# A gated attention and dense decode step on one Trainium2 core: the second weight load waits for a GpSimd fill

## The chip, the cores and the metric

The kernel runs on one core of one Trainium2 chip. The metric is the time of one execution on the device in microseconds (us), as the median of several runs. The profile is one further execution of the same program, taken by the hardware profiler.

## The reference, cut to what matters

All arrays are float32. A token of 512 features for each of two batch rows goes through a sliding block of attention over cached keys and values, and through a dense layer with Mish; a sigmoid gate mixes the two.

```python
W = min(4096, max(256, Sk // 4))              # Sk = 32768, so 4096 cached positions
q = (x @ wq) split into 32 heads of 128       # x: 2 x 512, wq: 512 x 4096
k, v = the last W positions of the caches, 8 kv heads, each for 4 query heads
p = softmax(q . k * 128 ** -0.5)
a = (p . v, heads joined) @ wo                # wo: 4096 x 512
h = x @ w1 + b1                               # w1: 512 x 1792
b = (h * tanh(softplus(h))) @ w2              # w2: 1792 x 512
g = sigmoid(sum(x * gate_w))
return g * a + (1 - g) * b
```

Nearly all bytes are the cached keys and values (8 kv heads of 8 MiB each) and the weights wq, wo, w1 and w2. Each is read once.

## The kernel before, in words

The work is one stream of loads from HBM into SBUF with the computation hung on it. Three buffers of 128 partitions x 16384 floats (8 MiB, the pool `stream`) take turns. The first holds all of `wq`, the next eight fills hold one kv head each (keys in the first half, values in the second), and the last two hold w1 with parts of w2 and wo (`w12`), and the rest of wo.

Nearly all loads are issued by SyncE, in the order in which `load` (L69 to L75) and the later lines call them, and each goes over the same hardware queue to the 16 DMA engines of the core. At the start SyncE issues:

- `wqh`, the first 2048 columns of `wq` (1 MiB; 8 KiB for each partition), at L73;
- `wqt`, the other 14336 columns (7 MiB; 56 KiB for each partition), at L73;
- `small`, 16 KiB with the token, the gate's weights and a bias, at L79, into the tile `sm`;
- the first two kv heads, at L73, into the two buffers that are still free.

The third kv head must wait until TensorE has used `wq` up, and each later load until the buffer that it takes has been read.

GpSimd starts with constants. In the order in which the program runs them: the identity matrix (masks.py), `ones` (L97), zeros for the padded token `x32` (L100; the profile calls the tile x), the first steps of a folding matrix (L87, L89), zeros for the padded queries `qz` (L103), more folding, zeros for `padded` (L106), and two small products of the folding matrix (L92, L111). Then it copies the token out of `sm` into `x32` (L101), for which it must wait for the load `small`, and multiplies token and gate weights (L118).

TensorE takes `x32` and `wq` to the queries (`queries`, L137), in two halves. VectorE puts them into the zeroed `qz` (L149). For each kv head follow the scores (L157), a maximum (L160), the exponentials (L162), a transposition (L169, L170) and the product with the values (L181). Behind the eighth head come the first layer of the dense part (`hidden`, L252), the output projections (L342) and, with the last load of w2, the final sums (L352). VectorE copies them to `res` (L385), and SyncE stores `res` (L386).

A scheduler places the instructions of each engine. Where `pin` (`tc.keep_in_program_order`) stands around an instruction, it keeps its place in the program's order.

Of the kernel before, what the change touches and what calls it, by code (L numbers as in the profile page):

```python
# [55 lines left out]
def decode_kernel(ctx: ExitStack, tc: tile.TileContext, res, stored, small, wqh, wqt, kv_in, w12, wo, w2, *rest):  # L56
    *parts, before, behind, out = rest
    nc = tc.nc
# [8 lines left out]
    loads = []  # L67

    def load(name, *parts):  # L69
        t = stream.tile([P, 2 * CHUNK], F32, tag="s", name=name)  # L70
        x = 0
        for cols, src in parts:
            loads.append(nc.sync.dma_start(t[:, x : x + cols], src))  # L73
            x += cols
        return t  # L75

    wq_t = load("wq", (HEAD, wqh), (2 * CHUNK - HEAD, wqt))
    sm = const.tile([P, SMALL], F32, name="sm")
    loads.append(nc.sync.dma_start(sm, small))  # L79
    xT = sm[:, : (DC + SLOTS) * B].rearrange("p (c b) -> p c b", b=B)  # L80
    gw = sm[:, (DC + SLOTS) * B : (DC + SLOTS) * B + DC]
    b1 = sm[:, (DC + SLOTS) * B + DC :]
# [17 lines left out]
    nc.gpsimd.memset(x32, 0.0)  # L100
    nc.gpsimd.tensor_copy(x32[:, :, ::RS], xT)  # L101
    qz = const.tile([P, HKV, BN * (Q + REP)], F32, name="qz")
    nc.gpsimd.memset(qz, 0.0)  # L103
    sizes = (HQ * Q, CUTS[1] * Q, (FC - CUTS[1]) * WIDE, WIDE)
    padded = const.tile([P, sum(sizes)], F32, name="padded")
    nc.gpsimd.memset(padded, 0.0)  # L106
# [182 lines left out]
    for kv in range(HKV):  # L289
        t = load(f"kv{kv}", (2 * CHUNK, kv_in[kv]))  # L290
        p = scores(kv, t[:, :CHUNK])
        ms = tops() if kv == HKV - 1 else None
        pT = turned(kv, p)
        values(kv, pT, t[:, CHUNK:], 0, 1)
        if kv == HKV - 1:
            kf, kl = factors(ms)
        values(kv, pT, t[:, CHUNK:], 1, 2)
        if kv == HKV - 1:
            r = shares(kl)
        values(kv, pT, t[:, CHUNK:], 2, NT)  # L300
    w12_t = load("w12", (AHEAD + CUTS[1] * D, w12))

    def flat(src, cuts, size):
# [4 lines left out]
    x = (WO[-1] - WO[0]) * REP * D  # L308
# [16 lines left out]
    x = 0  # L325
# [3 lines left out]
    x = AHEAD + CUTS[1] * D  # L329
# [31 lines left out]
    first = WO[0] * REP  # L361
# [19 lines left out]
    for ld in loads[-8:]:  # L381
        tc.add_manual_dep(landed.ins, ld.ins.name,
                          mybir.DependencyInfo(mybir.DependencyClass.Sync, mybir.DependencyReason.DATA),
                          reason="SyncE sees the last loads land ahead of the store")
# [5 lines left out]
                      reason="the store reads the copy")  # L390
# [72 lines left out]
```

## Time and profile before

| what | value |
|---|---|
| median of 3 runs | 218.84 us (218.77 to 218.93) |
| the profiled execution's own time | 219.24 us |
| its span, from the first instruction to the last | 217.4 us |
| bytes read from HBM | 91.24 MB |
| busy share of the span: TensorE, VectorE, ScalarE, GpSimd | 53%, 10%, 7%, 5% |
| mean granted TensorE clock | 0.867 |

The 219.24 us are the profiled execution timed as the runs are; the span lies inside it and leaves 1.84 us outside. Times in the views count from the span's start. The timeline shows a start, a duration, the engine, its source line and what is written from what; behind it, in brackets, the idle time of the engine and what ended it. SPq and POOLq are the queues of SyncE and GpSimd, on which DMA issues stand with the time that the engine needs to issue them, not with that of the transfer. The rows of windows give for a stretch of time its length, then the busy time of each engine with its count, the granted clock of TensorE, the busy share of the 16 DMA engines and the GB/s that they moved. A transfer is counted in the stretch in which it starts, with all its bytes, so short stretches go far above or below the mean once the pieces are large. The pieces of `wqh` are 8 KiB, and those of `wqt` 56 KiB.

### The profile page before, as it was taken

The page shows a single profiled execution, that of the slowest core. Times are in us where ns is not written, and L with a number is a line of the kernel's source. Part 1 is how long each engine was busy: PE and PEld are TensorE (multiplying, and loading weights), DVE is VectorE, ACT ScalarE, POOL GpSimd, SP SyncE. Part 2 cuts the span into 40 slices and gives each one's busy share as a digit, 9 for nine tenths or more (in the row PEclk, how much of TensorE's full clock was granted, in tenths as well). Part 3 has the DMA queues.
Part 4 walks back from the last instruction along what each step waited for, and adds up shares of the span by engine and source line. Part 5 has one row for each costly group of instructions (what it writes and reads, how often), then busy time and mean ns, then how long its engine had stood idle before and what let it go on. Part 6 is the DMA issues. An engine that isn't in the chain of part 4 may idle for free.

```text
span 217.4 us, 1857 instructions
## 1 busy us (share of the span) xinstructions
PE 115.5 (53%) x826; PEld 34.6 (16%) x826; DVE 21.5 (10%) x32; ACT 15.5 (7%) x34; POOL 11.4 (5%) x34
## 2 busy tenths in 40 slices
PE   0000798477046708543670754296165509669995
PEld 0000322112011102110210111012011101213333
DVE  0000000010001140100114010000501000260100
ACT  2000001111001100200110020002002000301001
POOL 8000000000000000000000000000000410100200
PEclk9999999979758995995898599769859976999799
DMA  8797988898899889998999899989998999989894
GB/s 362 338 507 338 582 386 386 386 570 386 386 398 567 386 377 410 543 398 386 410 497 434 386 422 458 470 386 422 437 482 386 434 449 421 427 377 475 381 409 162
DMA packets 2752, 91.38 MB, mean 420 GB/s; under 512 B 566, under 2 KB 646, under 8 KB 954
## 3 DMA queue, kind: packets, MB, share of 16 engines
q1 hardware_dynamic: 2602, 91.24, 97.4%
q8 instruction: 6, 0.10, 0.2%
q0 software_dynamic: 144, 0.05, 0.1%
HBM read 91.24 MB, written 0.04 MB: 420 GB/s over the span
## 4 chain that ended last, share of the span: by engine, by line
DMA 79%; PE 14%; ACT 2%; SPq 2%; DVE 1%; issue 1%; POOL 1%; ACTq 0%
DMA kv<-in_kv 61%; DMA w<-in_w 17%; PE sc L157 7%; PE o L181 5%; ACT p L162 1%; PE fin L352 1%; SPq L314 1%; DVE mx L160 1%; PE pp L169 1%; ACT pT L170 1%; POOL wo L310 1%; SPq L73 0%; SPq L327 0%; SPq L79 0%; DVE res L385 0%
## 5 line engine op out<-in xcount | busy, mean ns | idle before, releaser
L157 PE MATMUL sc<-kv,qz 128*32 128x512 f32 x256 | 44.6, 860 | 53.6 <-DMA kv<-in_kv 53.6
L181 PE MATMUL o<-kv,pT 128*32 128x512 f32 x256 | 29.5, 596 | 5.8 <-ACT pT L170 5.8
L137 PE MATMUL qp<-wq,x 128*32 128x512 f32 x64 | 12.1, 802 | 23.2 <-POOL x L101 23.2
L157 PEld LDWEIGHTS sc<-kv,qz 128*32 128x32 f32 x256 | 9.9, 151 | 87.6 <-DMA kv<-in_kv 60.2
L160 DVE TENSOR_REDUCE mx<-sc 128x1 f32<-128x512 f32 x8 | 5.5, 691 | 112.4 <-PE sc L157 112.4
L162 ACT ACTIVATE p<-sc,mx 128x512 f32<-128x512 f32 x8 | 5.5, 687 | 131.3 <-DVE mx L160 131.3
L169 PE MATMUL pp<-ident,p 128*128 128x128 f32 x32 | 5.2, 287 | 12.1 <-ACT p L162 12.1
L181 PEld LDWEIGHTS o<-kv,pT 128*32 128x32 f32 x256 | 7.3, 109 | 20.9 <-issue 13.2
L310 POOL MEMSET wo<- 128x1536 f32 x1 | 1.4, 1378 | 143.5 <-PE o L181 143.5
L191 DVE TENSOR_REDUCE od<-om 128x256 f32<-128x1024 f32 x4 | 7.6, 1911 | 0.1
L137 PEld LDWEIGHTS qp<-wq,x 128*32 128x32 f32 x64 | 2.5, 137 | 29.1 <-POOL x L101 23.2
L342 PE MATMUL acc<-wo,padded 128*32 128x512 f32 x56 | 7.1, 607 | 0.0
L188 DVE TENSOR_TENSOR om<-o,pick 128x1024 f32<-128x1024 f32 x4 | 4.9, 1224 | 19.3 <-PE o L181 19.3
L169 PEld LDWEIGHTS pp<-ident,p 128*128 128x128 f32 x32 | 3.4, 141 | 18.6 <-ACT p L162 18.6
L170 ACT COPY pT<-pp 128x512 f32<-128x512 f32 x8 | 4.7, 585 | 6.2 <-PE pp L169 6.2
L342 PE MATMUL acc<-w,padded 128*32 128x512 f32 x22 | 4.5, 884 | 0.4 <-DVE padded L235 0.4
L252 PE MATMUL hp<-w,x 128*32 128x512 f32 (+1 forms) x30 | 3.6, 540 | 1.8 <-DMA w<-in_w 1.8
L342 PEld LDWEIGHTS acc<-wo,padded 128*32 128x32 f32 x56 | 2.3, 117 | 4.6 <-issue 3.4
L252 PE MATMUL hp<-wo,x 128*32 128x512 f32 x6 | 2.7, 592 | 0.0
L126 DVE RECIPROCAL g<-g 128x2 f32<-128x2 f32 x1 | 0.2, 165 | 22.5 <-POOL g L125 22.5
L352 PE MATMUL fin<-w,padded 128*32 128x128 f32 x56 | 2.1, 277 | 0.3 <-DMA w<-in_w 0.3
L143 PE MATMUL qt<-ident,qs 128*128 128x128 f32 x8 | 1.3, 287 | 1.4 <-ACT qs L140 1.4
(71 smaller groups left out, 35.6 us busy)
## 6 DMA issues: line engine op xcount, KB each, us to landing
wq<-in_wqt SPq DMA_DIRECT2D x1, 7168.0 KB, 21.5
w<-in_w SPq DMA_DIRECT2D x1, 6144.0 KB, 40.6
wo<-in_wo SPq DMA_DIRECT2D x1, 5120.0 KB, 30.8
wo<-in_wo SPq DMA_DIRECT2D x1, 2048.0 KB, 35.2
wq<-in_wqh SPq DMA_DIRECT2D x1, 1024.0 KB, 5.0
w<-in_w SPq DMA_DIRECT2D x1, 1024.0 KB, 37.2
w<-in_w SPq DMA_DIRECT2D x1, 512.0 KB, 35.4
w<-in_w SPq DMA_DIRECT2D x1, 256.0 KB, 21.2
```

Of the source, the lines that this page charges most:

```text
L137: nc.tensor.matmul(qp[Q * k : Q * k + Q, :], x32[:, c, :], w[:, c, k, :], start=(c == 0), stop=(c == DC - 1))
L157: nc.tensor.matmul(sc[Q * j : Q * j + Q, :], qz[:, kv, m * Q : m * Q + Q], t[:, (m * NJ + j) * 512 : (m * NJ + j + 1) * 512], start=(m == ...
L160: nc.vector.tensor_reduce(mx[:, kv : kv + 1], sc, axis=AX.X, op=ALU.max, negate=True)
L162: nc.scalar.activation(p, sc, AF.Exp, bias=mx[:, kv : kv + 1], accum_out=ls[:, kv : kv + 1])
L169: pin(nc.tensor.transpose(pp[:, c, :], p[:, c * P : (c + 1) * P], ident))
L170: nc.scalar.copy(pT, pp)
L181: pin(nc.tensor.matmul(o[Q * j : Q * j + Q], pT[:, c, Q * j : Q * j + Q], t[:, (c * NJ + j) * 512 : (c * NJ + j + 1) * 512], start=(c == 0 ...
L188: nc.vector.tensor_tensor(ov, pair[0].rearrange("p k (m d) -> p k m d", m=BN), pick[:, None, :, None].to_broadcast([P, 2, BN, DH]), op=ALU ...
L191: nc.vector.tensor_reduce(od[:, kv - 1 : kv + 1], ov.rearrange("p k m d -> p k d m"), axis=AX.X, op=ALU.add)
L252: nc.tensor.matmul(hp[Q * j : Q * j + Q, :n], x32[:, c, :], w[:, :n], start=(c == 0), stop=(c == (DC + SLOTS if j in away else DC) - 1))
L342: return nc.tensor.matmul(acc[Q * j : Q * j + Q, :], lhsT, rhs, start=(n_col[j] == 1), stop=(n_col[j] == n))
L352: nc.tensor.matmul(fin[Q * j : Q * j + Q, :], lhsT[:, y : y + Q], rhs[:, j * P : (j + 1) * P], start=(done[0] == 0), stop=(done[0] == n_fi ...
```

## The change

SyncE issues `wqt`, the second load of `wq`, only when GpSimd has written the zeros of `qz`. The dependency is written for `loads[1:3]`, which are `wqt` and `small`; both also keep their places in the program's order, as all loads made by `load` now do.

```diff
         for cols, src in parts:
-            loads.append(nc.sync.dma_start(t[:, x : x + cols], src))
+            loads.append(tc.keep_in_program_order(nc.sync.dma_start(t[:, x : x + cols], src)))
             x += cols
...
     sm = const.tile([P, SMALL], F32, name="sm")
-    loads.append(nc.sync.dma_start(sm, small))
+    loads.append(tc.keep_in_program_order(nc.sync.dma_start(sm, small)))
...
     qz = const.tile([P, HKV, BN * (Q + REP)], F32, name="qz")
-    nc.gpsimd.memset(qz, 0.0)
+    blank = nc.gpsimd.memset(qz, 0.0)
+    for ld in loads[1:3]:
+        tc.add_manual_dep(ld.ins, blank.ins.name,
+                          mybir.DependencyInfo(mybir.DependencyClass.Sync, mybir.DependencyReason.DATA),
+                          reason="the first load has the queues for itself at first")
```

No instruction changes its place on any engine. On SyncE the one difference is a wait, at the start of the program, where `wq` and the first kv heads are loaded; lines marked - are the kernel before, lines marked + the changed one.

```order
 L73 DMA wq<-in_wqh 128x2048
-L73 DMA wq<-in_wqt 128x14336
+L73 DMA wq<-in_wqt 128x14336 [waits Pool_49]
 L79 DMA sm<-in_small 128x32
 L73 DMA kv_169<-in_kv 128x16384
```

Pool_49 is the semaphore that GpSimd counts up. Only `wqt` carries the wait; `small` and the first two kv heads stand behind it on SyncE and so come later too. On GpSimd the order in the changed kernel is that of before (behind the diff the line numbers are 4 higher):

```order
L100 MEMSET x_93 128x224
L87 TENSOR_TENSOR fold<-ident 128x32 [waits Pool_49]
L103 MEMSET qz 128x1152
L89 TENSOR_TENSOR fold<-fold,ident 128x32 [waits Pool_49]
L110 MEMSET padded 128x1744
L89 TENSOR_TENSOR fold<-fold,ident 128x32 [waits Pool_49]
L92 TENSOR_TENSOR key<-fold 128x8 [waits Pool_49]
L115 COPY padded<-fold 128x2
L101 COPY x_93<-sm 128x14 [waits DMAHW2_49]
```

The zeros of `qz` stand ahead of the copy that waits for `small`, so the two waits, SyncE's for GpSimd and GpSimd's for the load, don't close a circle.

## The prediction

> **What bounds the kernel now.** I began with the page's chain of the work that ended last, its shares by engine, and then the same chain in order of time (start, duration, what).
>
> ```profile
> DMA 79%; PE 14%; ACT 2%; SPq 2%; DVE 1%; issue 1%; POOL 1%; ACTq 0%
> ```
>
> ```profile
> 2.10 39.91 DMA kv<-in_kv
> ...
> 175.89 37.22 DMA w<-in_w
> 213.10 0.14 issue
> 213.24 2.25 PE fin L352 x64
> 215.49 0.03 issue
> 215.51 0.29 DVE res L385
> ```
>
> The chain is loads for four fifths of its length. It steps onto TensorE only where a buffer must be read before the next load is issued. Whether the loads really leave no gap there is read from the windows, over the whole middle of the span:
>
> ```profile
> 5.50:20.00 14.50, 0.00 (x0) 0.00 (x0) 0.00 (x0) 0.00 (x0) 0.00 (x0) 1.00 0.98 423
> 20.00:60.00 40.00, 24.71 (x148) 7.76 (x148) 1.43 (x6) 2.73 (x6) 0.77 (x4) 0.92 0.99 427
> 60.00:100.00 40.00, 20.33 (x136) 5.26 (x136) 4.49 (x4) 2.73 (x6) 0.00 (x0) 0.80 1.02 443
> 100.00:140.00 40.00, 19.24 (x136) 5.10 (x136) 4.49 (x4) 2.73 (x6) 0.00 (x0) 0.84 0.98 423
> 140.00:170.00 30.00, 18.58 (x128) 5.09 (x132) 4.49 (x4) 2.73 (x6) 0.00 (x0) 0.80 1.03 446
> 170.00:212.00 42.00, 29.54 (x214) 9.78 (x210) 6.17 (x12) 2.67 (x8) 6.11 (x15) 0.88 0.96 412
> ```
>
> The DMA share (last but one) stays between 0.96 and 1.03, and TensorE is busy for at most 0.70 of a row (29.54 of 42.00). So the kernel is one unbroken stream of loads, from about 2 us to 213.10, and then a tail: 217.4 - 213.1 = 4.3 us, in which the change touches nothing. The time moves by as much as the stream begins earlier or later, or by a hole in it, and by nothing else. All that matters is whether the change does one of these two in the first 6 us.
>
> **The wait's length.** Here are SyncE's issues at the start, and GpSimd's fill, from the timeline.
>
> ```profile
> 0.72 0.39 SPq L73 DMA_DIRECT2D wq<-in_wqh  x1
> 1.17 0.41 SPq L73 DMA_DIRECT2D wq<-in_wqt  x1
> ...
> 1.79 1.05 POOL L103 MEMSET qz<- 128x1152 f32 x1
> ```
>
> ```profile
> 1.62 0.43 SPq L79 DMA_DIRECT2D sm<-in_small  x1
> 2.10 0.77 SPq L73 DMA_DIRECT2D kv<-in_kv  x1
> ...
> 2.91 0.46 SPq L73 DMA_DIRECT2D kv<-in_kv  x1
> ```
>
> The fill ends at 1.79 + 1.05 = 2.84. What a wait of SyncE for a GpSimd fill costs beyond that is in the chain near the end, where a load waits for the fill at L310:
>
> ```profile
> 171.35 1.39 POOL wo L310
> 172.74 0.02 issue
> 172.75 0.89 SPq L314
> ```
>
> That is 0.02 us. So the issue of `wqt` moves from 1.17 to 2.86, by 1.69 us. Behind it on SyncE stand `small`, and the first two kv heads. With their own issue times kept (0.41, 0.43, 0.77, 0.46 and the gaps of 0.04 to 0.05 between them), `small` is issued at 3.3, the heads at 3.8 and 4.6. GpSimd doesn't wait for SyncE ahead of its copy of the token, so its fill isn't late.
>
> **What is queued behind the wait.** GpSimd waits for `small`, and TensorE for GpSimd's copy.
>
> ```profile
> 22.89 0.20 POOL L101 COPY x<-sm 128x14 f32<-128x14 f32 x1 [17.74 <-DMA sm<-in_small]
> ```
>
> `small` lands just ahead of 22.89 because 7 MiB of `wqt` stand ahead of it on the same queue, not because of its issue at 1.62. Issued at 3.3 it is still far ahead of its turn, and the first head, which follows it, too. The third head must wait until TensorE, which starts behind that copy, has used `wq` up, and so doesn't see the start. All this costs nothing as long as the queue holds `wqt` in time; what hides the 1.69 us is therefore `wqh` alone, the one load that is on the engines then.
>
> **Does `wqh` cover the wait?** Two things are needed: when the engines run out of `wqh`, and when they get `wqt`. The first is seen in short windows, since a piece of 56 KiB counted at its start lifts a slice far above the rate of the 8 KiB pieces.
>
> ```profile
> 4.70:4.80 0.10, 0.00 (x0) 0.00 (x0) 0.02 (x1) 0.00 (x0) 0.04 (x1) 1.00 1.35 573
> 4.80:4.90 0.10, 0.00 (x0) 0.00 (x0) 0.10 (x1) 0.00 (x0) 0.08 (x1) 1.00 1.71 737
> ...
> 5.30:5.40 0.10, 0.00 (x0) 0.00 (x0) 0.00 (x0) 0.00 (x0) 0.00 (x0) 1.00 2.66 1147
> 5.40:5.50 0.10, 0.00 (x0) 0.00 (x0) 0.00 (x0) 0.00 (x0) 0.00 (x0) 1.00 0.00 0
> ```
>
> The first engine goes over from `wqh` to `wqt` at 4.80 or just behind it, the last by 5.40; the middle is 5.10. The second is read from the two loads of the trace that find idle engines: `wqh` itself, and the store at the end.
>
> ```profile
> 1.60:1.70 0.10, 0.00 (x0) 0.00 (x0) 0.00 (x0) 0.10 (x1) 0.10 (x2) 1.00 0.00 0
> 1.70:1.80 0.10, 0.00 (x0) 0.00 (x0) 0.00 (x0) 0.10 (x1) 0.10 (x2) 1.00 0.42 164
> ```
>
> ```profile
> 215.83 0.35 SPq L386 DMA_DIRECT2D out<-res  x1
> ```
>
> ```profile
> 216.50:216.60 0.10, 0.00 (x0) 0.00 (x0) 0.00 (x0) 0.00 (x0) 0.00 (x0) 1.00 0.00 0
> 216.60:216.70 0.10, 0.00 (x0) 0.00 (x0) 0.00 (x0) 0.00 (x0) 0.00 (x0) 1.00 0.09 26
> 216.90:217.00 0.10, 0.00 (x0) 0.00 (x0) 0.00 (x0) 0.00 (x0) 0.00 (x0) 1.00 0.15 36
> ```
>
> From issue to first piece it is 1.70 - 0.72 = 0.98 to 1.08 us for `wqh`, and 216.60 - 215.83 = 0.77 to 0.87 us for the store. For `wqt`, issued at 2.86, that gives first pieces at 3.63 to 3.94, at least 0.86 us ahead of 4.80. But not all engines start at once, as the rate at the start shows:
>
> ```profile
> 1.50:2.00 0.50, 0.00 (x0) 0.00 (x0) 0.00 (x0) 0.50 (x1) 0.50 (x3) 1.00 0.19 66
> 2.00:2.50 0.50, 0.00 (x0) 0.00 (x0) 0.00 (x0) 0.00 (x1) 0.50 (x1) 1.00 0.31 82
> 2.50:3.00 0.50, 0.00 (x0) 0.00 (x0) 0.00 (x0) 0.00 (x0) 0.50 (x3) 1.00 0.76 295
> 3.00:3.50 0.50, 0.00 (x0) 0.00 (x0) 0.00 (x0) 0.00 (x0) 0.50 (x2) 1.00 0.97 410
> ```
>
> The full 410 GB/s are there only from 3.00, so the last engine may have got its first piece as late as 2.9, 2.2 us behind the issue. If `wqt` ramps up in the same way, its last engine gets work at 2.86 + 2.2 = 5.06. That is ahead of the middle, 5.10, and of 5.40, at which the last engine of `wqh` is through; the first engine of `wqh` would stand idle for 5.06 - 4.80 = 0.26 us only if it were the last one of `wqt`. I put the hole at 0, with 0.26 us as its upper bound. Without this cover the price would be the whole 1.69 us.
>
> **What the change can give.** In the kernel before the issues of `wqt`, `small` and the first head (1.17 to 2.87) fall into the slow ramp of `wqh`. By 3.00, (66 + 82 + 295) x 0.5 = 221 KB were moved, which take 0.54 us at 410 GB/s; since the first piece, 1.30 us had gone by. So 0.76 us of the stream are lost in the ramp. The changed kernel leaves `wqh` alone until 2.86. If the ramp comes from the issues behind it, up to 0.76 us come back; if it is the queue's own start, nothing does. The store, with nothing issued behind it, put all its pieces out from 216.60 to 217.00, which speaks for the first; but it runs at the end, on a queue long in use, and its pieces are small. Even in the better case `wqt` ramps up in its turn, now with `small` and the heads behind it: its last engine gets work at 5.06 in place of 5.40, a gain of 0.34, and its first engine can change over at 4.80 - 0.76 = 4.04, the full gain. The upper bound is the mean of the two, 0.55 us. I take 0.2 us, a little over half the way from 0 to the 0.34 us of the last engine: the last engine sets the end if all 16 carry the same bytes, as I assume, and the trace does not tell the two reasons apart.
>
> **The sum.** The profiled execution took 219.24 us. Less 0.2 for the ramp, plus 0 for the hole, it would be 219.04. It stands 0.40 us above the median of the runs (218.84), so the median of the changed kernel would be 218.64, say 218.65. That is 0.09% faster. About 0.2% (0.44 us) is what a measurement of this kernel can tell from no change, so I count my forecast as no change.
>
> **The rivals.**
>
> *The change does nothing.* Each engine has the pieces of `wqh` ahead of those of `wqt` on its list in any case, and the slice ahead of 4.80 (573 GB/s in 0.1 us, 7 pieces of 8 KiB) shows no piece of 56 KiB. Then `wqt` could not hold `wqh` up, the wait is hidden, and the time is 218.84. Against it stands only the slow ramp that coincides with the issues. The Trainium skill states a rule of this kind in "DMA: Bandwidth & Descriptors", under "Two DMAs through the same engine are not ordered": within one queue of one DMA engine, descriptors start in order. The trace agrees with it, by the slices around 4.80.
>
> *The ramp goes, and the gain is large.* With the full 0.55 us the time is 219.24 - 0.55 - 0.40 = 218.29; from a gain of 0.44 us on it counts as faster. For it speaks the issue time of the first head, 0.77 us where `wqt` and `small` took 0.41 and 0.43: something was held up in just this stretch. Against it speaks that the first pieces of `wqh`, in company, start 0.98 us behind their issue, little later than the 0.77 us of the store, and that `wqt` must ramp up as well. The landing of `wqh` gives a cross-check.
>
> ```profile
> wq<-in_wqh SPq DMA_DIRECT2D x1, 1024.0 KB, 5.0
> ```
>
> The Trainium skill, in "DMA: Bandwidth & Descriptors" under "Anatomy of one DMA", fits a load issued by GpSimd by itself as about 2.0 us and its bytes at 436 GB/s; as an estimate for this one that is 2.0 + 2.4 = 4.4 us, and the sum by it would be a gain of 0.6 us, where no run here shows `wqh` alone.
>
> *A hole between the two loads (slower).* Its place is the seam at 4.80 to 5.40. `wqt` is now prepared while the engines are busy, with `small` and two heads right behind it, and no row of this trace shows how long that takes with nothing else queued. If the ramp took twice as long as that of `wqh` (0.98 to the first piece, then 2 x 1.2 to the last engine), the last engine would have work at 2.86 + 3.38 = 6.24, a hole of 6.24 - 5.40 = 0.84 us, and the time would be 218.84 + 0.84 = 219.68. It decides against the change when the last engine's delay passes 5.40 + 0.44 - 2.86 = 2.98 us, against the 2.2 us seen. For it speaks only that the state isn't shown; against it the two idle-engine loads, both with a first piece within 1.08 us.
>
> **How the numbers follow.** My forecast, the wait hidden with a gain of under 0.44 us, has 0.45; that nothing happens, 0.23; the large gain, 0.20; the hole, 0.12. The first two both lie within 0.2%: 0.68. Faster by more, 0.20; slower by more, 0.12. The range begins at 218.25, just under the full gain, and ends at 219.10, which is 218.84 and the bound of the hole, 0.26; the slower rival and a little of the faster one stay out, under 2 in 10.
>
> **What would show it.** In the profile after, the issue of `wqt` should stand at about 2.86 with a wait for GpSimd at L103, the GB/s at 1.50 to 3.00 should be higher than before if the ramp came from the issues behind, the seam should lie at 4.6 to 5.4 with no slice of low rate ahead of it, the copy at L101 should start between 22.3 and 22.9, and all later landings should be moved by that amount. I am wrong if a stretch of 0.5 us between 3.0 and 5.5 falls clearly under 410 GB/s (the hole), if the copy at L101 comes over 0.4 us earlier (the large gain), or if it keeps its place and the end moves all the same, which would mean that the stream is disturbed later.

## The result, and the profile after

The changed kernel takes 219.34 us (median of 14 runs, 218.88 to 221.08) against 218.83 us for the kernel before (14 runs, 218.71 to 219.27). The ratio is 1.0026, with a 95% interval from 1.0013 to 1.0038: slower by 0.51 us. The runs also lie further apart than before, so what was added is not the same in each execution.

The profiled execution of the changed kernel took 219.28 us. It is near its median, while that of the kernel before (219.24) lies 0.4 us above its own. The two spans are both 217.4 us, so the two profiles don't show the 0.51 us as a difference in length; they show what differs at the start. SyncE's issues and the fill, from the timeline of the changed kernel:

```profile
0.73 0.39 SPq L73 DMA_DIRECT2D wq<-in_wqh  x1
1.80 1.05 POOL L103 MEMSET qz<- 128x1152 f32 x1
2.87 0.33 SPq L73 DMA_DIRECT2D wq<-in_wqt  x1
3.25 0.43 SPq L79 DMA_DIRECT2D sm<-in_small  x1
```

`wqt` is issued at 2.87 instead of 1.17, right behind the fill. The rates while `wqh` is read (windows; the last two columns are the share of the DMA engines and GB/s):

```profile
1.50:2.00 0.50, 0.00 (x0) 0.00 (x0) 0.00 (x0) 0.50 (x1) 0.50 (x3) 1.00 1.44 246
2.00:2.50 0.50, 0.00 (x0) 0.00 (x0) 0.00 (x0) 0.00 (x1) 0.50 (x1) 1.00 0.68 98
2.50:3.00 0.50, 0.00 (x0) 0.00 (x0) 0.00 (x0) 0.00 (x0) 0.50 (x2) 1.00 0.51 213
3.00:3.50 0.50, 0.00 (x0) 0.00 (x0) 0.00 (x0) 0.00 (x0) 0.50 (x2) 1.00 0.97 410
```

More pieces start ahead of 2.00 (246 GB/s against 66), but the share of 1.44 tells that they are long: 1.44 x 0.5 us x 16 engines are 11.5 us for 15 pieces of 8 KiB (246 GB/s over 0.5 us), 0.77 us each, where 410 GB/s on 16 engines make it 0.32. They began sooner and took longer. The full rate is there at 3.00, as before.

The next view shows what differs where the engines go over from `wqh` to `wqt`. The second pieces of `wqt`, 56 KiB each, begin when the first ones are done. One such piece in 0.5 us is 115 GB/s, so GB/s over 115 counts the pieces, and I take each for one engine, since the trace doesn't name the engine of a piece. Before:

```profile
6.50:7.00 0.50, 0.00 (x0) 0.00 (x0) 0.00 (x0) 0.00 (x0) 0.00 (x0) 1.00 0.26 115
7.00:7.50 0.50, 0.00 (x0) 0.00 (x0) 0.00 (x0) 0.00 (x0) 0.00 (x0) 1.00 3.97 1720
7.50:8.00 0.50, 0.00 (x0) 0.00 (x0) 0.00 (x0) 0.00 (x0) 0.00 (x0) 1.00 0.00 0
```

The changed kernel:

```profile
6.50:7.00 0.50, 0.00 (x0) 0.00 (x0) 0.00 (x0) 0.00 (x0) 0.00 (x0) 1.00 1.06 459
7.00:7.50 0.50, 0.00 (x0) 0.00 (x0) 0.00 (x0) 0.00 (x0) 0.00 (x0) 1.00 1.87 803
7.50:8.00 0.50, 0.00 (x0) 0.00 (x0) 0.00 (x0) 0.00 (x0) 0.00 (x0) 1.00 1.32 573
```

Before, 1 + 15 engines are done with their first piece by 7.50. In the changed kernel 4 engines are ahead of the rest, and 5 come behind 7.50. The trace's records of single transfers say why: around this place 16 pieces are under way but for 0.02 us, so no engine stands empty between the loads to speak of; the first pieces of `wqt` begin at 4.81 to 5.17 (before 4.85 to 5.33), but 7 of the 16 take 2.34 to 2.61 us, where the median piece has 2.12 and the longest first piece of before 2.26. They are drawn out. The last piece of `wqt` ends at 22.59 instead of 22.25, and `small` lands behind it.

```profile
wq<-in_wqt SPq DMA_DIRECT2D x1, 7168.0 KB, 20.0
wq<-in_wqh SPq DMA_DIRECT2D x1, 1024.0 KB, 4.8
sm<-in_small SPq DMA_DIRECT2D x1, 16.0 KB, 19.8
```

```profile
23.14 0.21 POOL L101 COPY x<-sm 128x14 f32<-128x14 f32 x1 [17.97 <-DMA sm<-in_small]
```

`wqh` lands 4.8 us behind its issue, 0.2 sooner than before. `wqt` has 1.70 us less for its bytes and needs only 1.5 us less (20.0 against 21.5). GpSimd's copy, which waits for `small`, starts at 23.14 instead of 22.89. Behind that the program runs as before; its last wait in the chain is still the same load, issued and landed within 0.1 us of where it stood, and the tail has the length it had:

```profile
175.88 37.28 DMA w<-in_w
213.17 0.14 issue
213.30 2.23 PE fin L356 x64
215.56 0.29 DVE res L389
```

### The profile page after: what moved, and what is told of

The parts are those of the page before. It is cut to its first block, busy times and chain, and to the rows that moved or that the text cites. A ratio compares the mean times of both kernels' runs of the same rounds, so it can differ in the third digit from the quotient of the medians.

```text
span 217.4 us, 1857 instructions
## 1 busy us (share of the span) xinstructions
PE 113.8 (52%) x826; PEld 33.6 (15%) x826; DVE 21.6 (10%) x32; ACT 15.5 (7%) x34; POOL 11.4 (5%) x34
## 4 chain that ended last, share of the span: by engine, by line
DMA 78%; PE 14%; ACT 2%; POOL 2%; SPq 2%; DVE 1%; issue 1%; ACTq 0%; POOLq 0%
DMA kv<-in_kv 61%; DMA w<-in_w 17%; PE sc L161 7%; PE o L185 5%; ACT p L166 1%; PE fin L356 1%; DVE mx L164 1%; SPq L318 1%; PE pp L173 1%; ACT pT L174 1%; POOL wo L314 1%; POOL qz L103 0%; SPq L331 0%; SPq L79 0%; DVE res L389 0%
## 5 line engine op out<-in xcount | busy, mean ns | idle before, releaser
L346 PE MATMUL acc<-wo,padded 128*32 128x512 f32 x56 | 6.4, 596 | 1.4 <-DMA wo<-in_wo 1.4
L346 PE MATMUL acc<-w,padded 128*32 128x512 f32 x22 | 2.8, 601 | 0.4 <-DVE padded L239 0.4
L346 PEld LDWEIGHTS acc<-wo,padded 128*32 128x32 f32 x56 | 1.6, 109 | 6.2 <-DMA wo<-in_wo 3.2
```

What stands on the lines that cost most here:

```text
L346: return nc.tensor.matmul(acc[Q * j : Q * j + Q, :], lhsT, rhs, start=(n_col[j] == 1), stop=(n_col[j] == n))
```

## The experiments

Theory A is that the wait costs at the seam, where the engines go over from `wqh` to `wqt`: `wqt` is issued too short a time ahead of it. Theory B puts the cost on the company, `small` and the two heads, which are now issued ahead of the seam too. C looks for it behind 23 us; D says that a wait there costs as such; G and H came up on the way. The kernel before was run again beside each of the five groups of experiments: its medians were 218.85 (x1 to x4), 218.89 (x5 to x8), 218.91 (x9 to x12), 218.90 (x13 to x16) and 218.86 us (x17, x18).

In what follows the *lead* of a kernel is the time from the issue of `wqt` to the start of its first piece on the first engine, in its profile. The *drawn-out* pieces are those of the 16 first ones that take over 0.15 us longer than the median piece, from the trace's records of single transfers.

**x1: the changed kernel again.** No edit.

> The changed kernel once more, for a second profile of it. Theory A (the seam): wqt, prepared late on busy engines, reaches the last engines late; some of its first 56 KiB pieces take 2.3 us and more where the kernel before has 2.12, the copy at L101 comes 0.2 to 0.6 us later than 22.89, and the median is again 219.1 to 219.6. Theory C (elsewhere): the copy at L101 stands within 0.1 us of 22.89 in this profile, and the time goes behind 23 us.

219.56 us (7 runs, 219.03 to 219.98), ratio 1.0031 (1.0019 to 1.0043). Two drawn-out pieces, the longest of 2.73 us; the copy at L101 starts at 23.43. As A has it; C, with the copy in its old place, falls.

**x2 and x3: the company alone, and `wqt` alone.** In x2 only `small` waits, with the heads behind it; in x3 `wqt` waits as in the change, and `small` for the next fill.

```diff
 x2
-    for ld in loads[1:3]:
+    for ld in loads[2:3]:
 x3
-    for ld in loads[1:3]:
+    for ld in loads[1:2]:
...
-    nc.gpsimd.memset(padded, 0.0)
+    blank2 = nc.gpsimd.memset(padded, 0.0)
+    for ld in loads[2:3]:
+        tc.add_manual_dep(ld.ins, blank2.ins.name, ...
```

> wqt is issued at 1.17 as in the kernel before, and only small, with the two heads behind it, waits for the zeros of qz. Theory A (the lateness of wqt itself at the seam costs): as before or a little under, 218.6 to 218.9, first pieces of wqt at 2.12 us. Theory B (the company costs: small and the heads, issued behind wqt while the engines are busy with wqh, hold up its pieces): still slower, 219.1 to 219.5, with the long first pieces of wqt.

> wqt waits for the zeros of qz as in the changed kernel, and small with the heads behind it waits for the next fill, padded, to about 4.55. Theory A: as slow as the changed kernel, 219.1 to 219.6, with long first pieces of wqt. Theory B: wqt is alone from 2.87 to 4.55 and is ready in time, so 218.6 to 218.9 and pieces of 2.12 us.

x2: 219.08 us, ratio 1.0012 (1.0003 to 1.0021), no drawn-out piece, copy at 22.74, and the profiled execution took 218.91. x3: 219.56 us, ratio 1.0031 (1.0019 to 1.0043), 5 drawn-out pieces. Taking the company away from `wqt` didn't help, and holding the company alone cost a third of what x1 lost (0.23 of 0.71 us). B falls as the cause. The 0.2 us of x2 fit neither theory well.

**x4: the wait made longer.** `wqt`, `small` and the heads wait for the fill of `padded`; the loop of the change stands behind it.

```diff
-    blank = nc.gpsimd.memset(qz, 0.0)
+    nc.gpsimd.memset(qz, 0.0)
...
-    nc.gpsimd.memset(padded, 0.0)
+    blank = nc.gpsimd.memset(padded, 0.0)
```

> wqt, small and the heads wait for the fill of padded, so wqt is issued at about 4.57, 1.70 us later than in the changed kernel. Theory A: the cover is gone, first pieces at 5.5 to 6.8 us instead of 4.8 to 5.2, and each further 0.1 us of wait costs 0.1 us: 220.6 to 221.1. Theory B: the same hole of the issue time alone, from 5.2 to about 5.6, and the held pieces, 219.7 to 220.3. Theory C: no more than the changed kernel, 219.3.

220.34 us, ratio 1.0067 (1.0055 to 1.0079): 1.5 us over before, under A's 220.6 and over B's 220.3 by little. Here there is a true hole (timeline, windows):

```profile
4.57 0.34 SPq L73 DMA_DIRECT2D wq<-in_wqt  x1
```

```profile
5.00:5.50 0.50, 0.00 (x0) 0.00 (x0) 0.00 (x0) 0.00 (x0) 0.17 (x2) 1.00 0.05 16
5.50:6.00 0.50, 0.00 (x0) 0.00 (x0) 0.00 (x0) 0.00 (x0) 0.00 (x0) 1.00 4.03 1262
6.00:6.50 0.50, 0.00 (x0) 0.00 (x0) 0.00 (x0) 0.00 (x0) 0.00 (x0) 1.00 1.14 459
```

```profile
24.26 0.21 POOL L101 COPY x<-sm 128x14 f32<-128x14 f32 x1 [19.09 <-DMA sm<-in_small]
```

Between 5.00 and 5.50 nearly nothing starts; the first pieces begin at 5.53 to 6.53, 0.96 to 1.96 us behind the issue, and 14 of 16 are drawn out, up to 3.20 us. The copy is 1.37 us late, about what the whole kernel loses. So here, on idle engines, a first piece begins 1 us behind the issue and then runs slowly.

**x5 and x6: shorter waits.** In x5 the loads wait for the zeros of `x32`, and no longer for those of `qz`; in x6 the zeros of `qz` are two fills, and the loads wait for the first.

```diff
 x5
-    nc.gpsimd.memset(x32, 0.0)
+    blank0 = nc.gpsimd.memset(x32, 0.0)
+    for ld in loads[1:3]:
+        tc.add_manual_dep(ld.ins, blank0.ins.name, ...
 x6
-    blank = nc.gpsimd.memset(qz, 0.0)
+    blank = nc.gpsimd.memset(qz[:, :4], 0.0)
+    nc.gpsimd.memset(qz[:, 4:], 0.0)
```

> wqt waits for the zeros of x32 instead, which end at about 1.62, so it is issued at about 1.65, 0.5 us later than before and 1.2 us sooner than in the changed kernel. Theory A, with 2.0 to 3.0 us from an issue until all engines run its pieces undisturbed: ready by 4.65 at the latest, ahead of nearly all of the seam, so no loss: 218.6 to 218.9, first pieces of wqt at 2.12 us. Rival D (any wait ahead of wqt costs, by its semaphore or by the order of the queue): slower by 0.3 us and more.

> The zeros of qz are written in two halves, and wqt waits for the first, so it is issued at about 2.35. Theory A: ready between 4.35 and 5.35, against a seam of 4.8 to 5.3, so next to nothing to 0.2 us is lost: 218.8 to 219.1, one or two long first pieces at most. Rival D: as slow as the changed kernel, 219.3 to 219.6.

x5, issue at 1.65: 218.88 us, ratio 0.9999 (0.9990 to 1.0008), no drawn-out piece. A wait ahead of `wqt` costs nothing as such, which is the end of D in its first form. x6, issue at 2.38: 219.88 us, ratio 1.0050 (1.0036 to 1.0064), slower than the change, where A expected 218.8 to 219.1. Five drawn-out pieces, one of 2.99 us. A was right on where the lateness is seen and wrong on the size of the loss. And the lateness doesn't go straight into the time: in the profiled execution the copy is 0.66 us late, and yet it took 219.13 us, the shortest of the five runs.

```profile
23.55 0.20 POOL L101 COPY x<-sm 128x14 f32<-128x14 f32 x1 [18.47 <-DMA sm<-in_small]
```

**x7 and x8: more cover.** The first load is made 2 MiB, with the change's wait (x7) and without any (x8).

```diff
-HEAD = 2048
+HEAD = 4096
```

> The changed kernel with a first load of 2 MiB instead of 1 MiB (HEAD 4096), so the seam lies about 2.5 us later, at about 7.5, and wqt, of 6 MiB in pieces of 48 KiB, is still issued at 2.87. Theory A: it is ready by 5.9, the cover is whole, and the loss is gone: 218.6 to 218.9, with all first pieces of wqt at 1.82 us. Rival D: still 219.2 to 219.6.

> The kernel before, without the wait, with the first load of 2 MiB: the control for the size alone. Theory A: 218.7 to 219.0, the same as the kernel before and as the 2 MiB load with the wait. If the wait itself gives something at the start, the kernel with the wait is up to 0.2 us faster than this one.

219.15 us (x7; ratio 1.0015, 1.0006 to 1.0024) and 219.18 us (x8; 1.0016, 1.0007 to 1.0024). Both lie above what A expected for them. The larger first load costs 0.3 us by itself (no piece is drawn out, and yet the copy starts at 23.34 and 23.36), and the wait then costs nothing: same wait, same issue time, a lead of 4.39 us instead of 1.94, and no drawn-out piece in either profile. This moved only the seam.

**x9, x10, x11: is it the split of the fill?** x9 waits for two of the eight parts of `qz`, x10 for the second half, x11 has the halves and no wait.

```diff
 x9
+    blank = nc.gpsimd.memset(qz[:, :2], 0.0)
+    nc.gpsimd.memset(qz[:, 2:], 0.0)
 x10
+    nc.gpsimd.memset(qz[:, :4], 0.0)
+    blank = nc.gpsimd.memset(qz[:, 4:], 0.0)
 x11 (on the kernel before)
+    nc.gpsimd.memset(qz[:, :4], 0.0)
+    nc.gpsimd.memset(qz[:, 4:], 0.0)
```

> wqt waits for the first two of the eight parts of the zeros of qz, written as a fill of its own, so it is issued at about 2.1, between the wait to 1.65 that cost nothing and the wait to 2.38 that cost 1.0 us. Theory A (wqt must be issued about 3 us ahead of the seam at 4.8 to 5.3): 2.7 to 3.2 us are left, so 0 to 0.5 us lost, 218.9 to 219.4. Theory G (the split of the fill costs, not the wait): 219.6 to 220.1, as with the halves.

> The fill of qz in halves, and wqt waits for the second half, so it is issued at about 3.05, as the changed kernel with the fill split. Theory A: as slow as the changed kernel or a little slower, 219.3 to 219.9. Theory G: slower than the wait for the first half, 220.0 and more.

> The kernel before with the fill of qz in halves and no wait: the control for the split. Theory A: 218.8 to 218.95, the same as before. Theory G: 219.3 and more.

x9, issue at 2.15: 219.90 us, ratio 1.0040 (1.0025 to 1.0054). x10, issue at 3.11: 219.34 us, ratio 1.0010 (0.9997 to 1.0024), which is not clear of no change; it has four drawn-out pieces, and the copy, at 22.85, is not late. x11: 218.91 us, ratio 1.0004 (0.9990 to 1.0017). The split costs nothing, and G, that the split is what costs, falls; but x9 misses A's 218.9 to 219.4. In its profiled execution (220.0 us) all 16 first pieces are drawn out, and the second ones start up to a microsecond late:

```profile
7.00:7.50 0.50, 0.00 (x0) 0.00 (x0) 0.00 (x0) 0.00 (x0) 0.00 (x0) 1.00 0.93 344
7.50:8.00 0.50, 0.00 (x0) 0.00 (x0) 0.00 (x0) 0.00 (x0) 0.00 (x0) 1.00 2.01 803
8.00:8.50 0.50, 0.00 (x0) 0.00 (x0) 0.00 (x0) 0.00 (x0) 0.00 (x0) 1.00 1.60 688
```

```profile
23.88 0.21 POOL L101 COPY x<-sm 128x14 f32<-128x14 f32 x1 [18.80 <-DMA sm<-in_small]
```

Three engines start at 7.0 to 7.5, seven at 7.5 to 8.0 and six later, where before 16 had started by 7.5. The copy is 0.99 us late.

**x12: a short lead with no wait.** The kernel before with a first load of 0.5 MiB.

```diff
-HEAD = 2048
+HEAD = 1024
```

> The kernel before, with no wait, but with a first load of half the size (HEAD 1024, 0.5 MiB, pieces of 4 KiB): the engines run out of wqh at about 3.6 to 4.1, some 2.4 to 2.9 us behind the issue of wqt at 1.17. Theory A (what counts is the time from the issue of wqt to the end of wqh, not the wait): first pieces of wqt (60 KiB, about 2.27 us) are drawn out by 0.2 us and more on some engines, and the median is 219.0 to 219.7. Theory D (the wait, its semaphore or the order on SyncE costs): 218.7 to 218.95, with no long pieces.

218.98 us, ratio 1.0002 (0.9991 to 1.0013): no loss. But 8 of the 16 first pieces are drawn out (2.43 to 2.57 us, the median piece 2.27), with a lead of 2.50 us and no wait anywhere. A holds for what makes pieces long and misses the time, so drawn-out pieces alone need not cost anything; the copy starts at 22.89, as before, and the last piece of `wqt` ends at 22.35 (before 22.25).

**x13, x14, x15, x16: why is a wait to 2.15 dearer?** x13 is x9 with the 2 MiB load; x14 is x9 with `small` held until the fill of `padded`; in x15 `small` alone waits to 2.15; in x16 the loads wait for the first step of the folding matrix instead of `qz`. H is that an issue between 2 and 3 us disturbs the engines in the ramp of `wqh`, whatever they do next.

```diff
 x13 (on x9)
-HEAD = 2048
+HEAD = 4096
 x14 (on x9)
-    for ld in loads[1:3]:
+    for ld in loads[1:2]:
...
+    blank2 = nc.gpsimd.memset(padded, 0.0)
+    for ld in loads[2:3]:
+        tc.add_manual_dep(ld.ins, blank2.ins.name, ...
 x15 (on x9)
-    for ld in loads[1:3]:
+    for ld in loads[2:3]:
 x16
+    blank3 = nc.gpsimd.tensor_tensor(fold, ident[:, :Q], ident[:, Q : 2 * Q], op=ALU.add)
+    for ld in loads[1:3]:
+        tc.add_manual_dep(ld.ins, blank3.ins.name, ...
```

> The wait to 2.15 (the first two parts of qz) with the first load of 2 MiB, whose seam lies at 7.3 to 8.3. Theory A (the cost arises at the seam, and cover takes it away): 219.0 to 219.3, as the 2 MiB load without a wait (219.18). Rival H (an issue between 2 and 3 us, in the ramp of wqh, disturbs the engines whatever they do next): 219.8 to 220.2.

> wqt waits for the first two parts of qz (issue at 2.15), and small with the heads behind it for the fill of padded (4.6). Theory B for this place (small and the heads, prepared right behind wqt and ahead of the seam, make the wait to 2.15 dearer than that to 2.87): 218.9 to 219.4. Theories A and H (wqt alone counts): 219.6 to 220.1, as with the wait to 2.15 for all.

> wqt is issued at 1.17, and only small with the heads behind it waits for the first two parts of qz, so small is issued at 2.15. Theory A: 218.8 to 219.1, with first pieces of wqt at 2.12 us. Rival H: 219.4 and more.

> wqt waits for the first step of the folding matrix, which ends at about 1.84, so it is issued at about 1.87, between 1.65 (no cost) and 2.15 (1.0 us). Theory A: 3.0 to 3.4 us ahead of the seam, at the edge: 218.85 to 219.4. Rival H (the harm begins at 2 us, when the engines are in their ramp): 218.8 to 218.95.

x13: 219.19 us, ratio 1.0014 (1.0005 to 1.0022), the time of the 2 MiB load without a wait. The dearer cost lies at the seam too, and H falls. x14: 219.98 us, ratio 1.0048 (1.0030 to 1.0065), 14 drawn-out pieces: not the company. x15: 218.91 us, ratio 1.0000 (0.9990 to 1.0009): again not the company. x16, issue at 1.87: 218.90 us, ratio 1.0003 (0.9994 to 1.0011). Its profiled execution happened to be the longest of its 11 runs, 219.61 us, where ten took 218.83 to 218.96; and it is one in which the seam went wrong:

```profile
6.50:7.00 0.50, 0.00 (x0) 0.00 (x0) 0.00 (x0) 0.00 (x0) 0.00 (x0) 1.00 0.59 229
7.00:7.50 0.50, 0.00 (x0) 0.00 (x0) 0.00 (x0) 0.00 (x0) 0.00 (x0) 1.00 3.32 1376
7.50:8.00 0.50, 0.00 (x0) 0.00 (x0) 0.00 (x0) 0.00 (x0) 0.00 (x0) 1.00 0.00 0
8.00:8.50 0.50, 0.00 (x0) 0.00 (x0) 0.00 (x0) 0.00 (x0) 0.00 (x0) 1.00 0.53 229
```

```profile
23.67 0.21 POOL L105 COPY x<-sm 128x14 f32<-128x14 f32 x1 [18.51 <-DMA sm<-in_small]
```

Two engines come behind 8.00, their first pieces drawn out to 3.00 and 2.81 us. The copy is 0.78 us later than in the kernel before, and this execution 0.71 us longer than the median of its kernel. Two late engines of 16 are enough to make the copy late: the last piece of `wqt` ends at 23.11 here, and `small`, for which the copy waits, lands behind it.

**x17 and x18: the lead of the change, mended.** The first load is made 1.5 MiB, with the change's wait (x17) and without (x18).

```diff
-HEAD = 2048
+HEAD = 3072
```

> The change's wait (issue of wqt at 2.87) with a first load of 1.5 MiB (HEAD 3072, pieces of 12 KiB), whose seam lies at about 6.0 to 6.7, so wqt is issued 3.1 to 3.8 us ahead of it. Theory A with a lead of 3 us: the cost is gone, and the time is that of the same size without the wait, within 0.15 us. If the wait itself costs whatever the lead: 0.5 us above it.

> The control for the size: a first load of 1.5 MiB without the wait. Between the kernel before (218.9) and the 2 MiB load without a wait (219.18): 218.85 to 219.2.

219.00 us (x17; ratio 1.0010, 1.0001 to 1.0019) and 218.90 us (x18; 1.0007, 0.9999 to 1.0016). With the issue at 2.87 as in the change and a lead of 3.07 us the wait costs 0.1 us, inside the intervals, and no piece is drawn out. No version tried is faster than the kernel before.

The kernel before, all kernels with a first load of 1 MiB in which `wqt` waits with the loads right behind it, and four in which the seam is elsewhere:

| kernel | issue of `wqt`, us | lead, us | drawn-out pieces | median, us |
|---|---|---|---|---|
| before | 1.17 | 3.68 | 0 | 218.83 |
| x5 | 1.65 | 3.10 | 0 | 218.88 |
| x16 | 1.87 | 2.90 | 3 | 218.90 |
| x9 | 2.15 | 2.72 | 16 | 219.90 |
| x6 | 2.38 | 2.50 | 5 | 219.88 |
| changed | 2.87 | 1.94 | 7 | 219.34 |
| x10 | 3.11 | 1.82 | 4 | 219.34 |
| x4 | 4.57 | 0.96 | 14 | 220.34 |
| x17 (1.5 MiB) | 2.87 | 3.07 | 0 | 219.00 |
| x7 (2 MiB) | 2.87 | 4.39 | 0 | 219.15 |
| x13 (2 MiB) | 2.15 | 5.16 | 0 | 219.19 |
| x12 (0.5 MiB) | 1.17 | 2.50 | 8 | 218.98 |

With a lead of 3.07 us and more no first piece is drawn out in any profile of the table, with 2.90 us and less some are in every one, wherever the seam lies and whether there is a wait or not. Of the kernels left out of it x1, x3 and x14 (leads of 2.00, 2.17 and 2.82 us; 2, 5 and 14 pieces) and x2, x8, x11 and x18 (3.36 us and more; none) fit in; x15, with 3.37 us, has one piece of 2.30 us, and the longest of the kernel before, 2.26 us, is just short of counting. So a lead of about 3 us is what it takes for undisturbed first pieces, with a soft edge. What the lateness then costs is not a function of the lead: with 1 MiB it is nothing at 2.90, 1.0 to 1.1 us at 2.82, 2.72 and 2.50, 0.4 to 0.7 at 1.82 to 2.17, and 1.5 at 0.96; with 0.5 MiB it was nothing that could be measured. Why the middle of the column is dearer than the change stays open (the intervals of x6, x9 and x14 overlap with that of the change, so this step is less sure than the loss itself); the split (x11), the company (x14) and the ramp (x13) are excluded. Open too is what happens inside a drawn-out piece, since the trace has its start and its duration and nothing in between.

## Why the prediction was wrong, point by point

**The stream as the bound** held in that, in the profile of the change, no gap opens behind the start. That the end moves by as much as the stream is late there was too simple. x4, x9 and x16 lose in whole (1.39, 1.09 and 0.71 us in their profiled executions, against the medians of the kernel before) about what the copy at L101 is late (1.37, 0.99 and 0.78 us). But x6's profiled execution is only 0.24 us longer, with a copy that is 0.66 us late. The profiled executions of the kernel before and of x15 are both 0.4 us above their medians, with the copy at 22.89. In the profile of the change the copy is 0.25 us late, and the median moved by 0.51.

**The wait's length** held: issue at 2.87 against 2.86 forecast, `small` at 3.25 against 3.3.

**What is queued behind the wait costs nothing**: held in x3, x14 and x15; x2 with its 0.2 us says that it is not quite proved.

**"I put the hole at 0, with 0.26 us as its upper bound" is the step that failed.** I took the delay to the last engine's first piece, 2.2 us, as all that a load needs, and compared it with the seam. The first pieces did begin in time, at 4.81 to 5.17, without an empty engine. But beginning is not running: issued 1.94 us ahead, 7 of the 16 were drawn out, and the median went up by 0.51 us where I had put the hole at 0. Counted to the first engine's going over, the need is about 3 us, and the change leaves 1.94. That too short a lead, behind a first load of 1 MiB, is the cause is shown: the loss goes when the same wait gets a lead of 3.07 us (x17 beside x18) or 4.39 us (x7 beside x8), and when the issue comes earlier (x5). By which path the lateness at the seam becomes the 0.51 us at the end stays open: x12 has eight drawn-out pieces and loses nothing, and x6 has a late copy in an execution that is hardly longer. The signs that I had named were not the right ones either: no row of 0.5 us between 3.00 and 5.50 fell clearly under 410 GB/s (the lowest has 377), and the copy came later than forecast, a case that I hadn't listed. A hint of it stood in rows that I had read: the ramp of `wqh`, in which pieces begin at 1.70 and the full rate comes at 3.00, 2.3 us behind the issue, may be this same effect at the start of the queue, which no run settles. I read it as engines without work. They were, for most of the row 2.00:2.50, with its share of 0.31; but the pieces that were under way were slow too (0.31 x 0.5 x 16 = 2.5 us for the 5 pieces that 82 GB/s are, 0.50 us each instead of 0.32).

**"I take 0.2 us" for the ramp** isn't borne out. In the profile of the change (246 + 98 + 213) x 0.5 = 278 KB were moved by 3.00 instead of 221, which is 0.14 us at 410 GB/s, and `wqh` landed 0.2 us sooner. But the same kernel's second profile, x1, has less:

```profile
1.50:2.00 0.50, 0.00 (x0) 0.00 (x0) 0.00 (x0) 0.50 (x1) 0.50 (x3) 1.00 1.07 131
2.00:2.50 0.50, 0.00 (x0) 0.00 (x0) 0.00 (x0) 0.00 (x1) 0.50 (x1) 1.00 0.39 115
2.50:3.00 0.50, 0.00 (x0) 0.00 (x0) 0.00 (x0) 0.00 (x0) 0.50 (x3) 1.00 0.58 229
```

That is 238 KB. Of the kernels that issue `wqt` at once, x11 moved 180 KB and x2 278. So the start differs that much from one execution to the next whatever is issued behind `wqh`, and no gain from leaving it alone is shown. The Trainium skill's fit, "DMA: Bandwidth & Descriptors" under "Anatomy of one DMA", which is for loads issued by GpSimd, gave 4.4 us as an estimate for `wqh` alone. With nothing issued behind it until 2.87 it took 4.8, and until 4.57 (x4) it took 4.9, so the gain of 0.6 us drawn from the fit is not there.

**The rivals.** The slower one, a hole between the two loads, had the right place and the right agent, and too low a chance (0.12). Its price (0.84 us) was nearer than my forecast; its form was not an empty engine, except in x4, for three engines in x9 and briefly in x14, but long pieces. That the change does nothing fell with the result. The row of 573 GB/s that I took for 7 pieces of 8 KiB has as many bytes as one piece of 56 KiB, so the rate alone didn't prove it; the single transfers do, the first piece of 56 KiB starts at 4.85. The rule of the Trainium skill that is cited there, that descriptors of one queue of an engine start in order ("DMA: Bandwidth & Descriptors", "Two DMAs through the same engine are not ordered"), is not at odds with these starts, and says nothing on how fast a piece runs once it has started.

## What to carry to other kernels

Issue a load well ahead of the moment when the queue runs out of the one in front of it, and measure "well" to the point at which its pieces run at full rate, not to their first start: here about 3 us on SyncE's queue, or, as an estimate, 1.2 MB of other loads at 410 GB/s. A wait that holds an issue back was free as long as about that lead was left (x5, x16, x7, x17). With less, behind a first load of 1 MiB, the median rose by 0.4 to 1.5 us, not in step with the lead. To see it, count how many pieces start in short windows one piece length behind the seam, before looking at idle time; and profile a kernel more than once, since one execution need not show what the median lost.

## What the runs showed of the hardware that was not expected

- Pieces issued late are drawn out without any gap ahead of them: 56 KiB took up to 2.61 us in the profile of the change, and up to 3.20 us in x4, where the median is 2.12.
- The first 15 pieces of 8 KiB of the very first load took 0.77 us on average in the changed kernel (0.32 at the full rate), with no other load issued; in its profile and in that of the kernel before, the rate was full from 3.00 on, 2.3 us behind the issue.
- An issue held back to 2.15 or 2.38 cost 1.0 us (x9, x6), and one to 2.87 only 0.5 us (0.7 in x1); at 3.11 (x10) the loss was not clear of no change.
- A first load of 2 MiB instead of 1 MiB, with all else the same, cost 0.3 us (x8: 1.0016, 1.0007 to 1.0024).
